# Moving the third chunk's inverse forward among the set-up work of a chunked RWKV-7 and GELU kernel

## Chip, core and metric

The kernel runs on one core of one Trainium2 chip, in fp32. The metric is the device time of one launch in microseconds (us). Five engines run their own queues in program order: PE (matrix multiply), DVE (vector), ACT (activations and copies), POOL (GpSimd) and SP, which here only issues transfers.

## What is computed

Two blocks follow each other. The first is a linear recurrence over 768 steps for 4 batches of 8 heads with a 40 x 40 state each, the second an MLP with exact GELU over 3072 tokens:

```python
for t in range(S):                                   # S = 768, state: (4, 8, 40, 40)
    y[:, :, t] = einsum('bhd,bhde->bhe', rt, state)
    Sa = einsum('bhde,bhe->bhd', state, at)
    state = state * wt[:, :, None, :] - einsum('bhd,bhe->bhde', Sa, bt)
    state = state + einsum('bhd,bhe->bhde', vt, kt)
x = y.transpose(0, 2, 1, 3).reshape(3072, 320)
h = x @ w_in                                          # 320 x 2048
out = (0.5 * h * (1 + erf(h / sqrt(2)))) @ w_out      # 2048 x 320
```

The two weight matrices arrive as 64-bit floats, so the kernel turns their words into fp32 itself, and this conversion is a large part of the set-up.

## The kernel before

**Chunks.** Time is cut into `NCH` = 12 chunks of 64 steps. Within a chunk the recurrence is solved by matrices. From the decays come `logs` (ACT, logarithm in place), `sums` (PE sums `cum` and `wT_ps`, then two exponentials on ACT), the scaled inputs `scale_b`, `scale_k`, `scale_a`, and their transposes `turn_a`, `turn_b`, `turn_k`, `turn_v`, `turn_r`. `make_N` multiplies the transposed a and b (`N_ps`), masks the product on DVE into `N` and writes its 32 x 32 blocks to DRAM. `start_inverse` fetches the blocks as `Nb` and inverts them column by column (L601, L603: two small elementwise operations for each of 31 columns), on DVE for chunk 0 and on POOL for the others. `store_inverse` and `fetch_inverse` take the result `W` through DRAM into `Tt` and `T2`; `turn_corner`, `corner` (`J`) and `joined` (the second `J`) complete it to 64 x 64. `make_A`, `make_av` and `make_RV` are further masked products. The serial part over the chunks is `make_X`, `make_sa`, `make_saT`, `make_y2`, `make_M`, `make_QY` and `outputs`, which writes the next state and the MLP's input `xt`.

**The MLP in pieces.** `mlp(c)` (L781) is a generator of eight pieces for each chunk: four pieces of the first layer (`ph`, one GELU on ACT each, into `gt`), then four of the second layer (`po`, 16 matmul records each; the first two pieces use rows 0 to 7 of `w_out_sb`, the last two rows 8 to 15). `fill()` puts the next piece of the oldest open chunk into PE's queue.

**Weight words.** `first_load` brings words of `w_in`, `first_convert` turns one (row block, half) into fp32: five pieces for the first half, five for the second. In this text they are called pieces 0 to 4 and h0 to h4. The first half's words wait in `w_out_sb` (not yet needed), the second half's in `gt` and `spare_raw`. `second_load` and `second_convert` do the same for the sixteen row blocks f0 to f15 of `w_out`. `to_float` (L281) uses DVE for the bit operations, ACT for a rescaling, and then either DVE or POOL for the last two operations; `power` and `mant` have two buffers each. `convert(n)` and `seconds(n, loads)` take the next n pieces from `queue`; a piece finished on DVE is begun one piece ahead.

**What sets the order.** The order on every engine is the order in which the program is written, by a manual schedule; there is no planner. L848 to L1012 are the set-up, written out by hand: chunks 0, 1 and 2 and the preparation of chunk 3, with conversions and MLP pieces of chunk 0 placed between. From L1014 a loop runs over c = 2 to 11, with eight `fill()` in each pass. Eight transfers can be open at once: each transfer issued by SP waits for the landing of the one eight earlier, as well as for its data and its target. PSUM has four tiles of the size `duo`, which all matrix results share.

**Names near the change.** `nb_ring`, `wp_ring`, `part_ring`, `avs_ring` hand out fixed buffers in turn. `raws` holds what was fetched. In the set-up before, chunk 2 is fetched by L886 (w) and L915, L916 (a, b); `sums(2)` is L940, `make_N(2)` L951, `run(start_inverse(2, ...))` L960; the first-half pieces are at L894 to L918, the second half's at L938 to L955; f0 to f15 at L966 to L1005; `store_inverse(2)` is L1000, `make_N(3)` L1007.

Of the kernel before, what the change touches and what calls it, by code (L numbers as in the profile page):

```python
# [19 lines left out]
def kernel(  # L20
# [197 lines left out]
    spare_raw = work.tile([P, 4 * DM], UINT32, tag="spare", name="spare_raw")  # L218
    early_a = spare_raw.bitcast(FP32).rearrange("p (n d) -> p n d", d=BW)

    for t in w_tile, early_w:
        nc.gpsimd.memset(t[:, G * DM:], 0.0)
    load_w(0)
# [137 lines left out]
    def second_load(f, slot, at=late_raw):  # L361
# [4 lines left out]
            to = second_raw[f] = at[:, slot * DM:(slot + 2) * DM]  # L366
        nc.sync.dma_start(out=to, in_=src[f * P:(f + 1) * P])

    def second_convert(f, eng):
        if wide_out:  # L370
            yield from to_float(w_out_sb[:, f], second_raw.pop(f), eng)
# [7 lines left out]
    def run(steps):  # L379
        for _ in steps:  # L380
            pass


    decays, turned_in = {}, {}
# [5 lines left out]
    def sums(c):  # L390
        logw = raws.pop((c, "w"))
        cum = duo("cum")[:, :, :DM]
        for g in range(G):
            mm(cum[:, g], cum_m, logw[:, g * DM:(g + 1) * DM])

        pt = duo("wT_ps").rearrange("p e (n t) -> p e n t", t=C)
        for n in range(G * NP):
            for x in range(2):
                for e in range(2):
                    at = (2 * n + x) * D  # L400
                    mm(pt[half(x), e, n], logw[half(e), at:at + HP], cum_m[half(e), half(e)])
        rw = (avs_ring if c in (1, 2) else part_ring)()[:, :, :DM]
        nc.scalar.activation(rw, cum, ACT.Exp, scale=-1.0)
        wp = wp_ring()
        nc.scalar.activation(wp[:, :, 1:].rearrange("p (n e) t -> p e n t", e=2), pt, ACT.Exp)
        decays[c] = rw.rearrange("p g (h d) -> p g h d", h=H), wp

# [11 lines left out]
    def side(name, tag, bufs):  # L419
        return work.tile([P, G, NP, P], FP32, tag=tag, name=name, bufs=bufs)  # L420
# [10 lines left out]

    def scale_b(c):
        rwv, wp = decays[c]
        nb = nb_ring()
        nc.vector.scalar_tensor_tensor(nb[:, :, :, :D], raws.pop((c, "b")), -1.0, rwv, ALU.mult, ALU.mult)
        turned_in.setdefault(c, {}).update(nb=nb, wp=wp)

# [20 lines left out]

    def turn_b(c):
        t = turned_in[c]  # L460
        nT = side("nT", "nT", 1)
        nc.scalar.copy(nT, flip(by_pair(t["nb"]), "nT_ps"))
        t["nT"] = parts(nT)

    def turns_a(c):
        turn_a(c)
        scale(c)
        scale_a(c)
        turn_b(c)

    def turn_k(c):
        t = turned_in[c]
# [3 lines left out]

    def turn_v(c):
        t = turned_in[c]
        vT = side("vT", "late", 1)
# [46 lines left out]

    blocks = {}

    def make_N(c):
# [9 lines left out]
        masked(flat(N), products("N_ps", t["nT"], t["aT"], True))  # L539
        blk = dram.tile([2, 2, 2 * G * NP, BL, BL], FP32, tag="N", name="N")  # L540
        for j in range(2):
            for z in range(2):
                at = j * HP + z * BL
                nc.sync.dma_start(out=blk[j, z].rearrange("n s t -> s n t"),
                                  in_=flat(N)[at:at + BL, :, z * BL:(z + 1) * BL])
        blocks[c] = blk
# [19 lines left out]
        t = turned_in[c]  # L566
        masked(flat(t["A"]), t.pop("A_ps"))

    def make_av(c):
        t = turned_in[c]  # L570
        av = duo("av")[:, :, :G * NP * D].rearrange("p x (g i d) -> p x g i d", g=G, i=NP)
        for g, i, x, e, q, m in units():
            mm(av[half(e ^ x), x, g, i], t["A"][half(e), x, g, i], t["VR"][half(e), g, q, m, :D])
        avs = t["avs"] = avs_ring()
        nc.scalar.copy(avs[:, :, :DM], av.rearrange("p x g i d -> p x (g i d)"))  # L575


    inverses = {}
# [107 lines left out]
    def make_sa(c):  # L686
# [176 lines left out]
    turn_b(1)  # L863
    scale_k(0)
    make_N(1)

    spare_x = work.tile([P, NK, TB], FP32, tag="xt", name="spare_x").rearrange("p k t -> p (k t)")
    st_ring()
# [25 lines left out]
    first_pieces((0,), 0, nc.vector)  # L894
    convert(1, True)
    mask_A(1)
    logs(2)
    first_load(True, 0, early(4))
    first_load(False, 2, early(5, 4))
    corner(0)  # L900
    joined(0)
    first_pieces((1, 2), 0, nc.gpsimd)
    first_pieces((3,), 0, nc.vector)
    first_pieces((4,), 0, nc.gpsimd)
    convert(1, True)
    make_X(0)
    make_sa(0)
    make_saT(0)
    convert(1, True)
    make_y2(0)  # L910
    make_M(0)
    store_inverse(1)
    load_r(1)
    fetch_inverse(1)
    load_a(2)  # L915
    fetch(2, "b", b, nc.sync)  # L916
    first_load(False, 3)
    convert(1, True)  # L918
    make_QY(0)
    outputs(0)  # L920
    pieces.append(mlp(0))
    make_av(1)
    corner(1)
    convert(1, True)
    joined(1)
    turn_state()
    make_X(1)
    turn_v(1)
    turn_r(1)
    make_RV(1)  # L930
    for f in range(2):
        second_load(f, 2 * f)
    first_load(True, 1, spare_raw[:, :LW])
    fetch(2, "k", k, nc.sync)
    for f in range(2, 8):
        second_load(f, 2 * f)

    first_pieces(range(NK), 1, nc.gpsimd)  # L938
    convert(1)
    sums(2)  # L940
    convert(1)
    make_sa(1)
    make_saT(1)
    scale_b(2)
    turn_a(2)
    scale_a(2)
    convert(1)
    fill()
    turn_b(2)
    fill()  # L950
    make_N(2)  # L951
    convert(1)
    make_y2(1)
    make_M(1)
    convert(1, True)  # L955
    scale_k(2)
    nc.gpsimd.memset(spare_st.rearrange("p e i g d -> p (e i g) d")[:, :, D:], 0.0)
    for n in "av":
        unused(paired[n], nc.gpsimd)
    run(start_inverse(2, nc.gpsimd))  # L960
# [12 lines left out]
    outputs(1)  # L973
    pieces.append(mlp(1))
    turn_v(2)
# [8 lines left out]
    fetch(3, "k", k, nc.sync)  # L984
    load_VR(3)
    load_a(3)
    seconds(1, (11, 14))
    fill()
    seconds(1, (12, 0, spare_raw))
    seconds(1, (13, 2, spare_raw))  # L990
    make_av(2)
    sums(3)
    scale(3)
    turn_a(3)
    scale_a(3)
    turn_state()
    fill()
    seconds(2, (14, 14))
    turn_b(3)
    store_inverse(2)  # L1000
    fetch_inverse(2)
    seconds(1, (15, 0, spare_raw))
    load_r(3)
    load_v(3)
    seconds(2, last=True)  # L1005
    fill()
    make_N(3)  # L1007
    run(start_inverse(3, nc.gpsimd))
    turn_k(3)
    turn_r(3)  # L1010
    turn_corner(2)
    fill()  # L1012
# [87 lines left out]
```

## Time and profile before

| what | value |
|---|---|
| time, median of 3 runs | 774.02 us (770.8 to 774.39) |
| the profiled execution | 767.67 us, span on the core 765.9 us |
| PE matmul busy | 699.2 us, 91% of the span |
| DVE, ACT, POOL busy | 277.8, 218.7, 311.5 us |
| mean granted PE clock | 0.95 |
| bytes moved | 67.82 MB in 268361 packets |

The profiled execution is 3.1 us below the fastest of the three timed runs. The page's first part gives each engine's busy time; its second cuts the span into 40 slices of 19.1 us, a digit for tenths busy, with PE's granted clock in a row of its own. Other views used below are the stretches (busy time of each engine between two times), the waits (who waited for whom), the timeline (instructions in order of time) and the chain of work that ended last. "<-" after a name reads "from": in `Tt<-inv` the tile `Tt` is loaded from `inv`, and "[6.62 <-DVE A L507]" says that the engine sat idle for 6.62 us until a DVE instruction of line 507 ended.

### The profile page before, as it was taken

Reading aid. Unit: us, or ns where it says so; the run is one execution under the profiler, and the core shown is the slowest. Engines: PE = TensorE matmul, PEld = TensorE weight load, DVE = VectorE, ACT = ScalarE, POOL = GpSimd, SP = SyncE. Lnnn points to the kernel's source line nnn. Section 1 sums busy time; section 2 is a strip of 40 time slices with the busy share of each in tenths; the row PEclk is TensorE's granted clock in tenths of the full one; section 3 lists DMA queues with packets and bytes.
Section 4 is the critical chain, followed back from the end, with each engine's and each line's share of the span. In section 5 each row is a group of like instructions: output and inputs, shape, how many; then the busy total and the mean of one; then the engine's idle time right before and its main releaser. Section 6 shows DMA issues by size and latency. Waiting matters only on the chain.

```text
span 765.9 us, 30557 instructions
## 1 busy us (share of the span) xinstructions
PE 699.2 (91%) x13792; PEld 561.3 (73%) x13792; DVE 277.8 (36%) x420; ACT 218.7 (29%) x262; POOL 311.5 (41%) x778
## 2 busy tenths in 40 slices
PE   7346787676999999999999999999999999999997
PEld 5346676454887877877878878878878878778684
DVE  3777456963143143243252242341241431321000
ACT  5124653340331331341332322322322413102020
POOL 3384248820750750841832823814804706500000
PEclk9666999886999999999999999999999999999999
DMA  9896565465725635535537337237347241110100
GB/s 117 137 174 133 117 195 98 89 127 120 128 45 99 117 69 101 100 66 115 94 59 130 72 68 142 58 69 135 63 76 138 50 74 38 34 36 3 27 9 17
DMA packets 268361, 67.82 MB, mean 89 GB/s; under 512 B 256616, under 2 KB 261512, under 8 KB 268232
## 3 DMA queue, kind: packets, MB, share of 16 engines
q1 hardware_dynamic: 268032, 65.71, 45.9%
q8 instruction: 108, 1.77, 1.0%
q14 instruction: 21, 0.17, 0.1%
q10 hardware_dynamic: 200, 0.16, 0.1%
HBM read 51.68 MB, written 10.22 MB: 81 GB/s over the span
## 4 chain that ended last, share of the span: by engine, by line
PE 77%; POOL 7%; SPq 5%; issue 5%; DMA 4%; DVE 1%; ACT 0%; POOLq 0%; DVEq 0%; ACTq 0%
PE po L797 26%; PE ph L789 26%; PE QY L100 5%; PE J L100 2%; PE N_ps L100 2%; POOL tmp L601 1%; POOL W L603 1%; PE sap L100 1%; PE X L100 1%; DMA a_pairs<-in_a_dram 1%; POOL st L603 1%; PE saT_ps L100 1%; PE kT_ps L413 1%; PE nT_ps L413 1%; PE cum L100 1%
## 5 line engine op out<-in xcount | busy, mean ns | idle before, releaser
L797 PE MATMUL po<-w_out_sb,gt 128*128 128x320 f32 x768 | 223.8, 444 | 17.0 <-DVE w_out_sb L297 15.3
L789 PE MATMUL ph<-xt,w_in_sb 64*128 64x256 f32 x1920 | 223.7, 385 | 5.3 <-POOL w_in_sb L302 4.8
L789 PEld LDWEIGHTS ph<-xt,w_in_sb 64*128 64x128 f32 x1920 | 184.9, 189 | 29.6 <-POOL w_in_sb L302 5.6
L797 PEld LDWEIGHTS po<-w_out_sb,gt 128*128 128x128 f32 x768 | 144.0, 193 | 79.7 <-DVE w_out_sb L297 20.6
L601 POOL TENSOR_TENSOR tmp<-W,Nb 128x126 f32<-128x126 f32 (+22 forms) x310 | 111.6, 360 | 172.8 <-DMA Nb<-N 149.2
L603 POOL TENSOR_TENSOR W<-W,tmp 128x126 f32<-128x126 f32 (+22 forms) x310 | 118.6, 383 | 24.3
L791 ACT ACTIVATE gt<-ph 128x1024 f32<-128x1024 f32 x48 | 49.2, 1024 | 166.3 <-PE ph L789 166.2
L801 DVE COPY os<-po 128x320 f32<-128x320 f32 x24 | 11.8, 491 | 108.7 <-PE po L797 108.7
L507 DVE TENSOR_TENSOR SM<-M_ps,upper 128x1024 f32<-128x1024 f32 x12 | 14.7, 1224 | 67.6 <-PE M_ps L100 67.5
L591 POOL MEMSET W<- 128x512 f32 x10 | 5.3, 530 | 73.8 <-DMA inv<-W 73.8
L746 DVE TENSOR_TENSOR xt<-QY,wpT 128x512 f32<-128x512 f32 x24 | 15.4, 685 | 51.3 <-PE QY L100 51.3
L668 DVE COPY Tt<-J 32x512 f32<-32x512 f32 x12 | 8.3, 689 | 67.5 <-ACT Tt L668 67.5
L474 ACT COPY kT<-kT_ps 128x1024 f32<-128x1024 f32 x12 | 12.1, 1011 | 70.9 <-PE kT_ps L413 70.9
L507 DVE TENSOR_TENSOR VR<-RV_ps,upper 128x1024 f32<-128x1024 f32 x12 | 14.7, 1222 | 43.1 <-PE RV_ps L100 43.1
L441 POOL TENSOR_TENSOR ks<-k_raw,part 128x640 f32<-128x640 f32 x10 | 16.2, 1617 | 32.5 <-DMA k_raw<-in_k_dram 17.2
L507 DVE TENSOR_TENSOR A<-A_ps,upper 128x1024 f32<-128x1024 f32 x12 | 14.6, 1220 | 39.4 <-PE A_ps L100 39.4
L289 ACT ACTIVATE power<-power,rebias 128x320 uint32<-128x320 uint32 (+1 forms) x26 | 16.0, 622 | 44.8 <-DVE power L288 44.8
L791 ACT ACT_TABLE_LOAD x10 | 12.8, 1283 | 43.6 <-PE ph L789 43.6
L575 ACT COPY avs<-av 128x640 f32<-128x640 f32 x12 | 8.3, 693 | 53.5 <-PE av L100 53.5
L100 PE MATMUL QY<-SM,nb 64*64 64x104 f32 x768 | 21.3, 263 | 1.3 <-DVE SM L507 1.3
L100 PEld LDWEIGHTS QY<-SM,nb 64*64 64x64 f32 x768 | 18.7, 140 | 5.1 <-issue 3.6
L100 PEld LDWEIGHTS av<-VR,A 64*64 64x64 f32 x768 | 13.9, 149 | 11.6 <-DVE A L507 6.8
(152 smaller groups left out, 878.0 us busy)
## 6 DMA issues: line engine op xcount, KB each, us to landing
Nb<-N SPq DMA_DIRECT2D x22, 256.0 KB
VR<-in_v_dram SPq DMA_DIRECT2D x24, 160.0 KB
out_dram<-os SPq DMA_DIRECT2D x48, 80.0 KB
w_tile<-in_w_dram SPq DMA_DIRECT2D x22, 160.0 KB
b_raw<-in_b_dram SPq DMA_DIRECT2D x22, 160.0 KB
k_raw<-in_k_dram SPq DMA_DIRECT2D x22, 160.0 KB
w_out_sb<-in_moe_w_out_dram SPq DMA_DIRECT2D x11, 320.0 KB
N<-N SPq DMA_DIRECT2D x48, 64.0 KB
```

The source lines that it names most:

```text
L100: nc.tensor.matmul(o, lhsT, rhs, start=first, stop=True, skip_group_check=True)
L289: nc.scalar.activation(power, power, ACT.Relu, bias=rebias, scale=8.0)
L413: nc.tensor.transpose(pt[:, g, n], src(g, n), ident)
L441: eng.tensor_tensor(ks[:, :, :, :D], raws.pop((c, "k")), rwv, ALU.mult)
L474: nc.scalar.copy(kT, flip(by_pair(t["ks"]), "kT_ps"))
L507: nc.vector.tensor_tensor(to, pt, upper.unsqueeze(1).to_broadcast([P, 2 * G * NP, C]), ALU.mult)
L601: eng.tensor_tensor(t, W[:, :rows, j:j + 1].to_broadcast([P, rows, rest]), Nb[:, j:j + 1, j + 1:].to_broadcast([P, rows, rest]), ALU.mult)
L603: eng.tensor_tensor(W[:, :rows, j + 1:], W[:, :rows, j + 1:], t, ALU.add)
L746: nc.vector.tensor_tensor(xt[:, :NP, g * P:(g + 1) * P].rearrange("p i (e t) -> p i e t", e=2), Y, wp[:, g, :, :, :C], ALU.mult)
L789: nc.tensor.matmul(ph[:, x, s], w_in_sb[half(x), kt, p * P:(p + 1) * P], xt[half(x), kt], start=kt == 0, stop=kt == NK - 1)
L791: nc.scalar.activation(gt[:, 4 * q:4 * q + 4].rearrange("p (x s) t -> p x s t", x=2), ph, ACT.Gelu)
L797: nc.tensor.matmul(po[:, g], gt[:, f, g * P:(g + 1) * P], w_out_sb[:, f], start=f == 0, stop=f == NF - 1)
```

## The change

Line numbers are those of the kernel before. The change touches the order of the set-up and some buffers.

- Chunk 2's decays, transposes and `N` product move forward. `load_w(2)`, `load_a(2)` and `fetch(2, "b")` are issued ahead of the first weight words; `logs(2)`, `sums(2)`, `turn_a(2)` stand ahead of `run(inverse)`, the rest (`scale_b`, `turn_b`, `scale_a`, the product of `make_N`) between `fetch_inverse(0)` and `corner(0)`. Two temporary buffers hold its results: `wp_2` in `spare_raw` and `nb_2` in the tile of `a`. `move(2)` copies them into the rings later, on ACT. The exponential for chunk 2 goes to `part_ring`; chunk 1's `make_X` writes over its `avs`.
- All four parts of the first half's words are issued later, the first after `fetch_inverse(0)`. All five first-half pieces are finished on POOL, and all stand after `make_M(0)`.
- The inverse of chunk 2 is started before the first conversions and its 31 columns are spread: 10 after piece 4, 2 after h1, the rest after h4.
- Three more loads of `w_out` words (f10, f11, f15) get buffers of their own. Two `fill()` of the set-up are taken away, and f14 and f15 are converted in the loop's first pass.
- `make_N(3)` now stands ahead of `store_inverse(2)`, and `store_inverse(2)` and `fetch_inverse(2)` directly ahead of chunk 3's `start_inverse`.
- In the loop's first pass two second-layer pieces of chunk 0 come after `make_saT(2)`, with pieces of chunk 1's first layer ahead of them (`pieces.reverse()`), and the pass has ten `fill()`.

```diff
+    wp_2 = spare_raw.bitcast(FP32)[:, :G * NP * 2 * (C + 1)].rearrange("p (n t) -> p n t", t=C + 1)
+    nb_2 = by_64(paired["a"]).rearrange("p (g h) d -> p g h d", g=G)
...
+    def columns(n):
+        for _ in range(n):
+            next(later, None)
...
-        rw = (avs_ring if c in (1, 2) else part_ring)()[:, :, :DM]
+        rw = (avs_ring if c == 1 else part_ring)()[:, :, :DM]
-        wp = wp_ring()
+        wp = wp_2 if c == 2 else wp_ring()
...
-        nb = nb_ring()
+        nb = nb_2 if c == 2 else nb_ring()
...
+    def move(c):
+        t = turned_in[c]
+        nb, wp = nb_ring(), wp_ring()
+        nc.scalar.copy(nb[:, :, :, :D], t["nb"][:, :, :, :D])
+        nc.scalar.copy(wp[:, :, 1:], t["wp"][:, :, 1:])
+        t["nb"], t["wp"] = nb, wp
+        decays[c] = decays[c][0], wp
...
-        xs = t["xs"] = part_ring()
+        xs = t["xs"] = t["avs"] if c == 1 else part_ring()
...
-    fetch(1, "k", k, nc.sync, ahead["k"])
+    load_w(2)
     load_VR(0)
     load_r(0)
-    first_load(False, 0, early(0, 4))
-    first_load(False, 1)
+    load_a(2)
+    fetch(2, "b", b, nc.sync)
     turn_k(0)
     make_A(0, False)
+    logs(2)
     turn_v(0)
     turn_r(0)
     make_RV(0, False)
+    sums(2)
+    turn_a(2)
     run(inverse)
     store_inverse(0)
-    load_VR(1)
-    load_w(2)
+    fetch(1, "k", k, nc.sync, ahead["k"])
     fetch_inverse(0)
+    mask_A(0)
+    scale_b(2)
+    make_av(0, False)
+    turn_b(2)
+    scale_a(2)
     scale_k(1, nc.vector)
-    mask_A(0)
+    copy_av(0)
     mask_RV(0)
-    make_av(0)
+    make_N(2, False)
     turn_k(1)
     make_A(1, False)
-    first_pieces((0,), 0, nc.vector)
-    convert(1, True)
     mask_A(1)
...
+    first_load(False, 0, early(0, 4))
+    store_inverse(1)
+    first_load(False, 1)
     corner(0)
     joined(0)
+    mask_N(2)
+    load_VR(1)
+    first_pieces(range(NK), 0, nc.gpsimd)
     make_X(0)
     make_sa(0)
     make_saT(0)
+    fetch_inverse(1)
+    first_load(True, 0, early(4))
+    later = start_inverse(2, nc.gpsimd)
+    first_load(False, 2, early(5, 4))
     make_y2(0)
     make_M(0)
+    convert(2)
     make_QY(0)
     outputs(0)
     pieces.append(mlp(0))
     make_av(1)
     corner(1)
+    convert(1)
     joined(1)
+    move(2)
+    convert(1)
     turn_state()
     make_X(1)
+    convert(1, True)
+    first_load(False, 3)
+    load_r(1)
...
+    columns(10)
+    first_pieces(range(NK), 1, nc.gpsimd)
+    make_sa(1)
+    make_saT(1)
+    convert(1)
+    fill()
+    convert(1)
+    fill()
+    turn_v(1)
+    turn_r(1)
+    make_RV(1)
+    columns(2)
+    convert(1)
     make_y2(1)
     make_M(1)
+    convert(2, True)
     scale_k(2)
...
+    columns(BL)
...
+    second_load(10, 0, words("b_raw"))
+    second_load(11, 0, words("k_raw"))
+    second_load(15, 0, words("rT", 2))
     second_pieces(range(NF), nc.vector)
-    seconds(3)
+    seconds(2)
     fill()
     turn_k(2)
+    make_QY(1)
     fill()
-    seconds(3)
-    make_QY(1)
+    seconds(2)
     outputs(1)
...
     load_w(3)
-    fetch(3, "b", b, nc.sync)
-    seconds(2, (10, 12))
-    logs(3)
...
+    seconds(4, (12, 12))
     load_VR(3)
     load_a(3)
+    logs(3)
     make_av(2)
     sums(3)
+    seconds(1, (13, 14))
+    fill()
+    seconds(3)
+    fetch(3, "b", b, nc.sync)
+    fetch(3, "k", k, nc.sync)
+    turn_a(3)
+    turn_state()
+    seconds(2, (14, 14), last=True)
     scale(3)
     scale_a(3)
+    turn_b(3)
     fill()
+    make_N(3)
     store_inverse(2)
     fetch_inverse(2)
+    run(start_inverse(3, nc.gpsimd))
...
     for c in range(2, NCH):
         corner(c)
         make_X(c)
+        if c == 2:
+            pieces.reverse()
+            seconds(2, last=True)
+            turn_r(n)
         fill()
...
         make_saT(c)
+        if c == 2:
+            pieces.reverse()
+            fill()
         fill()
         make_y2(c)
         make_M(c)
+        if c == 2:
+            fill()
```

More of the change, by code (lines that the diff above doesn't have):

```diff
@@ L367, in second_load, with words @@
         nc.sync.dma_start(out=to, in_=src[f * P:(f + 1) * P])
+    def words(tag, bufs=1):
+        return work.tile([P, 2 * DM], UINT32, tag=tag, name="words", bufs=bufs)
     def second_convert(f, eng):
@@ L460, in turn_b @@
         t = turned_in[c]
-        nT = side("nT", "nT", 1)
+        nT = side("nT", "late" if c == 2 else "nT", 1)
         nc.scalar.copy(nT, flip(by_pair(t["nb"]), "nT_ps"))
         t["nT"] = parts(nT)
[L465 to L469, printed above, removed]
+    def move(c):
[5 more added lines that the diff above has]
+        decays[c] = decays[c][0], wp
     def turn_k(c):
@@ L478, in turn_v @@
         t = turned_in[c]
-        vT = side("vT", "late", 1)
+        vT = side("vT", "kT" if c == 1 else "late", 1)
         if c < NT:
@@ L527, with make_N, mask_N @@
     blocks = {}
-    def make_N(c):
+    def make_N(c, mask=True):
+        t = turned_in[c]
+        t["N_ps"] = products("N_ps", t["nT"], t["aT"], True)
+        if mask:
+            mask_N(c)
+    def mask_N(c):
         t = turned_in[c]
@@ L538, in make_N @@
         t["N"] = N
-        masked(flat(N), products("N_ps", t["nT"], t["aT"], True))
+        masked(flat(N), t.pop("N_ps"))
         blk = dram.tile([2, 2, 2 * G * NP, BL, BL], FP32, tag="N", name="N")
@@ L567, in mask_A, with make_av @@
         masked(flat(t["A"]), t.pop("A_ps"))
-    def make_av(c):
+    def make_av(c, copy=True):
         t = turned_in[c]
@@ L573, in make_av, with copy_av @@
             mm(av[half(e ^ x), x, g, i], t["A"][half(e), x, g, i], t["VR"][half(e), g, q, m, :D])
+        t["av_ps"] = av.rearrange("p x g i d -> p x (g i d)")
+        if copy:
+            copy_av(c)
+    def copy_av(c):
+        t = turned_in[c]
         avs = t["avs"] = avs_ring()
-        nc.scalar.copy(avs[:, :, :DM], av.rearrange("p x g i d -> p x (g i d)"))
+        nc.scalar.copy(avs[:, :, :DM], t.pop("av_ps"))
     inverses = {}
@@ L865 @@
     make_N(1)
+    nc.gpsimd.memset(wp_2[:, :, 0], 1.0)
     spare_x = work.tile([P, NK, TB], FP32, tag="xt", name="spare_x").rearrange("p k t -> p (k t)")
@@ L882 @@
     make_RV(0, False)
+    sums(2)
+    turn_a(2)
     run(inverse)
     store_inverse(0)
-    load_VR(1)
-    load_w(2)
+    fetch(1, "k", k, nc.sync, ahead["k"])
     fetch_inverse(0)
+    mask_A(0)
[3 more added lines that the diff above has]
+    scale_a(2)
     scale_k(1, nc.vector)
-    mask_A(0)
+    copy_av(0)
     mask_RV(0)
-    make_av(0)
+    make_N(2, False)
     turn_k(1)
     make_A(1, False)
-    first_pieces((0,), 0, nc.vector)
-    convert(1, True)
     mask_A(1)
-    logs(2)
-    first_load(True, 0, early(4))
-    first_load(False, 2, early(5, 4))
+    first_load(False, 0, early(0, 4))
+    store_inverse(1)
+    first_load(False, 1)
     corner(0)
     joined(0)
[L902 to L905, printed above, removed]
+    mask_N(2)
+    load_VR(1)
+    first_pieces(range(NK), 0, nc.gpsimd)
     make_X(0)
@@ L908 @@
     make_saT(0)
-    convert(1, True)
+    fetch_inverse(1)
+    first_load(True, 0, early(4))
+    later = start_inverse(2, nc.gpsimd)
+    first_load(False, 2, early(5, 4))
     make_y2(0)
     make_M(0)
[L912 to L918, printed above, removed]
+    convert(2)
     make_QY(0)
@@ L923 @@
     corner(1)
-    convert(1, True)
+    convert(1)
     joined(1)
+    move(2)
+    convert(1)
     turn_state()
     make_X(1)
+    convert(1, True)
+    first_load(False, 3)
+    load_r(1)
+    first_load(True, 1, spare_raw[:, :LW])
+    for f in range(2):
+        second_load(f, 2 * f)
+    fetch(2, "k", k, nc.sync)
+    for f in range(2, 8):
+        second_load(f, 2 * f)
+    columns(10)
[5 more added lines that the diff above has]
+    convert(1)
+    nc.gpsimd.memset(spare_st.rearrange("p e i g d -> p (e i g) d")[:, :, D:], 0.0)
+    fill()
     turn_v(1)
@@ L930 @@
     make_RV(1)
[L931 to L951, printed above, removed]
+    columns(2)
     convert(1)
@@ L954 @@
     make_M(1)
-    convert(1, True)
+    convert(2, True)
     scale_k(2)
-    nc.gpsimd.memset(spare_st.rearrange("p e i g d -> p (e i g) d")[:, :, D:], 0.0)
     for n in "av":
         unused(paired[n], nc.gpsimd)
-    run(start_inverse(2, nc.gpsimd))
+    columns(BL)
     load_VR(2)
@@ L980 @@
     load_w(3)
-    fetch(3, "b", b, nc.sync)
-    seconds(2, (10, 12))
-    logs(3)
-    fetch(3, "k", k, nc.sync)
+    seconds(4, (12, 12))
     load_VR(3)
     load_a(3)
[L987 to L990, printed above, removed]
+    logs(3)
     make_av(2)
     sums(3)
+    seconds(1, (13, 14))
[6 more added lines that the diff above has]
+    seconds(2, (14, 14), last=True)
     scale(3)
-    turn_a(3)
     scale_a(3)
-    turn_state()
+    turn_b(3)
     fill()
-    seconds(2, (14, 14))
-    turn_b(3)
+    make_N(3)
     store_inverse(2)
     fetch_inverse(2)
-    seconds(1, (15, 0, spare_raw))
+    run(start_inverse(3, nc.gpsimd))
     load_r(3)
     load_v(3)
[L1005 to L1008, printed above, removed]
     turn_k(3)
-    turn_r(3)
     turn_corner(2)
-    fill()
     for c in range(2, NCH):
```

## The prediction

> **What bounds the kernel now.** I read the slices first, then stretches, PE's waits, and the timelines of PE, POOL and SP.
>
> ```profile
> PE   7346787676999999999999999999999999999997
> PEclk9666999886999999999999999999999999999999
> ```
>
> PE and its clock reach 9 in the eleventh slice (about 191 us) and stay there. So only the set-up can win or lose. The stretches (busy us of PE, PEld, DVE, ACT, POOL; clock; DMA share; GB/s) show how:
>
> ```profile
> 44.00:62.00 18.00, 6.40 (x224) 5.68 (x228) 11.96 (x20) 4.72 (x6) 14.10 (x34) 0.60 0.78 143
> 62.00:97.00 35.00, 26.43 (x953) 23.46 (x944) 21.86 (x33) 18.88 (x30) 10.81 (x9) 0.84 0.69 138
> 97.00:133.00 36.00, 29.71 (x500) 24.54 (x502) 21.48 (x35) 15.71 (x23) 22.56 (x37) 0.93 0.61 144
> 133.00:193.00 60.00, 42.73 (x582) 28.91 (x578) 39.10 (x77) 17.50 (x24) 21.85 (x47) 0.77 0.57 112
> ```
>
> After 97 us, PE's longest waits are for converted weights:
>
> ```profile
> PE po L797 <- DVE w_out_sb L297: 15.3, 7, 6.7
> PE ph L789 <- POOL w_in_sb L302: 4.8, 2, 3.1
> ```
>
> The timeline gives the marks that I move (start, duration):
>
> ```profile
> 42.65 1.16 PE L100 MATMUL RV_ps<-rT,vT 40*64 40x64 f32 x64 [1.10 <-ACT rT L495]
> 50.43 1.95 PE L100 MATMUL av<-VR,A 64*64 64x40 f32 x64 [6.62 <-DVE A L507]
> 60.12 1.08 PE L100 MATMUL J<-L,N 32*32 32x32 f32 x64 [3.54 <-DVE L L638]
> 138.72 1.15 PE L100 MATMUL A_ps<-aT,kT 40*64 40x64 f32 x64
> 191.83 1.14 PE L100 MATMUL X<-st,aT 40*64 40x40 f32 x64
> ```
>
> X of chunk 2 ends at 193.0; from there PE is full to the end. My method: find when the changed kernel ends that X, add PE work that it still owes there. Eight MLP pieces are done by then before, six after, so two second-layer pieces (4.50 and 4.31 in the chain's rows at 218.85 and 227.48) are owed: +8.8. The change must therefore end X by 184.2 to break even.
>
> **What the Trainium skill says.** "TensorE: Matmul & The Clock Gate", Part 1: an idle PE falls to half clock and needs sustained work to return. The trace agrees: 0.60 in 44 to 62, and `QY` from `SM` took 3.05 at 71.65 but 1.66 at 129.79. "SBUF — State Buffer", Who interferes with whom: a DVE instruction with two SBUF inputs contends with a GpSimd instruction that reads SBUF. It agrees: a second-layer conversion starts every 2.74 (142.65 to 145.39) beside POOL's columns, every 1.93 (163.13 to 165.06) without. "ScalarE: Activation LUTs", What ACT_TABLE_LOAD costs: 1283 ns for any set; here 1.28. "DMA: Bandwidth & Descriptors", Anatomy of one DMA: about 2 us fixed, on the GpSimd path; on SP's the chain shows 2.02 for a block store of `N` and 3.40 for `inv`.
>
> **Part 1: chunk 2's N in the wait.** PE idles from 43.8 to 50.4. But `sums(2)` can't start there: in the changed order `cum` waits for chunk 0's A mask, which empties the PSUM tile it takes, and that mask stands behind DVE's inverse (done 48.3). So the new work starts at 49.4 and lies on the way to the first J, not beside it. Durations from before's rows, slow ones because the clock was 0.53:
>
> - PE: cum 2.5 (154.02) to 52.0; wT_ps 1.4 to 53.5; a's flips 2.0 (as kT at 52.30) to 55.3.
> - ACT beside it: table 1.28, exponentials 0.70 and 1.03, to 55.0.
> - DVE: `scale_b` writes into a's tile, so it waits for the flips: 0.83 to 56.2; `scale_a` to 57.3, `scale_k(1)` 1.05 to 58.3, RV mask to 59.4.
> - PE: av to 57.2, b's flips to 58.7, ACT copy 1.0 to 59.7, N to 61, k's flips 2.0 to 62.8, copy to 63.9, A to 65.3; DVE mask 1.2 and corner transpose 0.7 to 67.2.
>
> J starts at 67.3 instead of 60.12: +7. With all these at full clock (cum 1.34, flips 1.04 and so on) I get +3; with another table load and slow products +9. I take +7. The moved `N` (1.2), flips and sums cost PE nothing later; before they sat at 88 to 109 between waits, so little is won there.
>
> SP: the first words are issued after `fetch_inverse(0)`, at about 55.5 instead of 37.1; w, a and b of chunk 2 (0.98 MB in all) and k of chunk 1 take their place. Behind that queue the fourth words part is issued at 95 instead of 80.5, landing by an estimated 102 (before 7 to 8 after issue).
>
> **Part 2: first half on POOL.** J's second product, sap, saT, M follow as before, 7 later; QY ends at 83 (76.3). Pieces 0 and 1 run beside QY. Then DVE and ACT take turns: one piece holds DVE 1.5, ACT 1.9 to 2.0, POOL 2.65 (L301 1.29 and L302 1.35). `move(2)` adds 0.7 and 1.0 on ACT, ahead of piece 3 on that queue. POOL ends piece 4 at about 99.3 (before 84.8). The first two `ph` still end near 106.4 (before 107.9), because sums, a, b and RV work no longer precede them.
>
> **Part 3: columns between conversions.** Ten columns take POOL 8.5 (before, 8.1 quiet at 31.88 and 9.4 at 124.11), to 107.8. h0 follows to 110.5. The first GELU writes where h0's words lie, so it waits for POOL at 109.1; behind it in ACT's queue stand h1's rescaling, then the v and r copies, for which RV waits. h1 ends at 114.9, two columns (2.0) at 117.3. RV at 116.6, its mask to 119, h2 to 124.5, h3 to 128, h4 to 130.7. Before h4 ended at 119.1. The other 19 columns run 134 to 155.5; before the inverse ended at 155.2. So the inverse is not earlier; the conversions are 11.6 later. The third `ph` waits for h4: it ends at 133.3, QY(1) at 137.6 (132.9), the fourth `ph` 142.5, A of chunk 2 148.8 (139.9): +9.
>
> **Part 4: the second layer's conversions.** Before, f0 to f4 were done ahead of `xt`; now f0 to f2, as f0 needs the `mant` buffer h3 leaves. DVE idles for RV until 147.8; masks and a memset to 151.1. Then f3 and f4 at 2.7, f5 to f10 at 1.93: 168.1. Transpose of a 1.25; f11 to f13 5.3 to 174.6; `scale_b(3)` to 175.4. PE meanwhile waits: `sums(3)` needs `logs(3)`, which is behind f7's rescaling on ACT, so PE idles some 9 us before 160; the word load for f12 holds SP until f6 is done, but what stands behind it (v, a) lands in time. The buffers for f10, f11 and f15 remove before's 6.26 wait for `spare_raw` (timeline at 177.56); DVE is late for another reason, so I book nothing more. After `scale_b(3)`: flips 1.1, one po piece 4.5, N 1.1, mask to 183.5.
>
> **Part 5: N(3) ahead of the inverse's store.** Before:
>
> ```profile
> 166.87 1.28 SPq L615 DMA_DIRECT2D inv<-W  x2
> 170.94 1.93 SPq L625 DMA_DIRECT2D Tt<-inv  x4
> 185.51 1.93 SPq L544 DMA_DIRECT2D N<-N  x4
> ```
>
> The fetch was long over at J(2). Now SP waits for the N(3) mask, writes N (1.93), stores (1.28, 3.4 to land), fetches (two of four needed, 2.8 to land), and DVE transposes 0.7: 9.5 after the mask. PE has only k's flips (1.1) in that time. J(2) 193, X ends at 194.9.
>
> **Sum.** X is +1.9; the two owed pieces +8.8; after a 10 us wait PE is slow again, +0.8 (the po piece after before's wait took 5.33, not 4.50). Total +11.5. Against its own execution: 767.67 + 11.5 = 779.2. That execution is 6.35 below the median of its runs, so the same difference on 774.02 gives 785.5. From the bounds, J +3 to +9, POOL's columns 8.1 to 9.4, the fetch 8 to 12 and an uncertainty of some 4 in the DVE chain give 778 to 793.
>
> **Rivals.**
>
> 1. *Faster.* POOL had room: in 60 to 121 it waited 19.3 and 16.0 for ACT's `mant`. If the twelve columns (10.5) fit into such waits and J is only 3 late, h4 ends at 116, not 130.7. Each microsecond of h4 is one of N(3) and X, so X ends about 14.5 earlier; f3 and f4 without POOL beside them save 1.6: total -4.5, 769.5. It decides for faster when h4 ends before about 119. Against it: POOL waits for ACT because ACT waits for DVE and for GELU, and the program puts ten columns in one block ahead of h0.
> 2. *Level.* h4 ends near 119 to 122 and the inverse's fetch lies partly beside po: 774.
> 3. *Much slower.* The words are the bound: the fourth part lands after 108 and the second layer's loads queue behind it. DVE starts h0 some 6 later and every following step with it: +18, 792; with the longer J bound 797.
> 4. *It does not do what it says*, that is, the wait of the first transfers is not used: this is inside my forecast, since `cum` waits for DVE.
>
> **Numbers.** Forecast 60%, much slower 12%, level 14%, faster 14%. Likeliest time 785.5, its own range 778 to 793. For 8 in 10 I reach down to 772 (some 10% beneath) and up to 797. A measurement of this kernel can tell 0.5%, 3.9 us, from no change: faster 0.14, same 0.14, slower 0.72.
>
> **What would show it.** J of chunk 0 at 67 rather than 60; L302's fifth run on POOL at 98 to 100; h4 at 131; a PE wait of about 9 us for DVE's L just before J(2), which before was hidden; X(2) ending near 195; po no longer waiting for L297 by more than a few us. I am wrong if h4 ends before 122, if J(2) follows N(3) directly, or if PE is full before 185.

## The result, and the profile after

The changed kernel takes 794.4 us, median of 4 runs (791.01 to 796.12), against 773.52 us (4 runs, 770.8 to 774.39) for the kernel before: a ratio of 1.0271, 95% interval 1.0227 to 1.0314. That is 20.9 us slower, where 11.5 were forecast. Its profiled execution took 793.85 us (span 792.0), near its median. In later series the kernel before ran between 767.83 and 777.87 us (one run of 783.74 at a lower clock is left out), so its profiled 767.67 was at the fast end of its runs; that is why the spans differ by 26.1 us and the medians by 20.9.

The slices of the changed kernel, as on its page:

```profile
PE   7366666854799999999999999999999999999997
PEclk9676785968699999999999999999999999999999
```

A slice is 19.8 us here. PE is at 9 from the twelfth slice on, and the loss lies ahead of that. The same stretches as before (busy us of PE, PEld, DVE, ACT, POOL; clock; DMA share; GB/s):

```profile
44.00:62.00 18.00, 10.83 (x284) 8.53 (x272) 10.04 (x18) 4.80 (x6) 15.10 (x39) 0.81 0.56 108
62.00:97.00 35.00, 21.91 (x850) 20.15 (x854) 19.98 (x28) 15.79 (x26) 11.56 (x12) 0.70 0.66 136
97.00:133.00 36.00, 23.85 (x393) 19.95 (x386) 12.13 (x19) 15.15 (x22) 22.71 (x36) 0.69 0.70 157
133.00:193.00 60.00, 38.44 (x590) 30.39 (x592) 40.58 (x83) 19.83 (x27) 22.02 (x46) 0.76 0.35 81
```

The first stretch did fill: PE 10.83 instead of 6.40. The three behind it hold 14.7 us less PE work in all (84.2 against 98.9), and the clock in 97 to 133 fell from 0.93 to 0.69. PE's longest waits after 97 us:

```profile
PE J L100 <- DVE L L664: 9.3, 1, 9.3
PE nT_ps L424 <- DVE nb L446: 8.6, 1, 8.6
PE cum L100 <- ACT w_tile L399: 8.0, 1, 8.0
PE RV_ps L100 <- ACT rT L509: 5.7, 2, 4.6
PE ph L815 <- POOL w_in_sb L305: 5.1, 2, 3.8
```

Before, PE waited for converted second-layer weights (15.3 us in seven waits). That is gone; in its place stand three waits of 8 to 9 us: `cum` for chunk 3's logarithm, the flips of b (`nT_ps`) for its scaled b, and J for chunk 2's corner. The marks, from PE's timeline:

```profile
66.00 1.08 PE L100 MATMUL J<-L,N 32*32 32x32 f32 x64 [1.96 <-DVE L L664]
153.97 1.11 PE L100 MATMUL A_ps<-aT,kT 40*64 40x64 f32 x64
203.83 1.08 PE L100 MATMUL J<-L,N 32*32 32x32 f32 x64 [9.25 <-DVE L L664]
204.84 1.95 PE L100 MATMUL X<-st,aT 40*64 40x40 f32 x64
206.71 7.40 PE L815 MATMUL ph<-xt,w_in_sb 64*128 64x256 f32 x40
```

What J waited for is in SP's queue. The three kinds of transfer that the prediction's part 5 shows now stand in the other order, the inverse's store and fetch behind the blocks of `N`:

```profile
194.88 1.94 SPq L564 DMA_DIRECT2D N<-N  x4
196.91 1.28 SPq L641 DMA_DIRECT2D inv<-W  x2
200.51 1.90 SPq L651 DMA_DIRECT2D Tt<-inv  x4
```

X of chunk 2 ends at 206.8 instead of 193.0: 13.8 us. The rest of the span is longer too, as the stretches from the end of X to the end show, the kernel before first, then the changed one:

```profile
193.00:765.90 572.90, 566.98 (x11080) 458.58 (x11080) 157.61 (x194) 146.51 (x166) 222.48 (x590) 1.00 0.39 74
```

```profile
206.80:792.00 585.20, 578.34 (x11112) 465.51 (x11112) 163.70 (x207) 148.15 (x168) 223.94 (x590) 1.00 0.39 75
```

The 32 additional matmul records are the two owed pieces. 13.8 + 12.3 = 26.1, the whole difference of the spans. In what follows, "the rest" is this stretch from the end of X of chunk 2 to the end.

### The profile page after: what moved, and what is told of

The parts are those of the page before. It is cut to its first block, busy times and chain, and to the rows that moved or that the text cites. A ratio compares the mean times of both kernels' runs of the same rounds, so it can differ in the third digit from the quotient of the medians.

```text
span 792.0 us, 30573 instructions
## 1 busy us (share of the span) xinstructions
PE 704.3 (89%) x13792; PEld 568.2 (72%) x13792; DVE 273.0 (34%) x416; ACT 222.5 (28%) x268; POOL 314.6 (40%) x783
## 4 chain that ended last, share of the span: by engine, by line
PE 78%; POOL 5%; DMA 5%; DVE 4%; SPq 3%; issue 3%; ACT 2%; POOLq 0%; DVEq 0%; ACTq 0%
PE ph L815 27%; PE po L823 26%; PE QY L100 6%; PE J L100 2%; PE cum L100 2%; POOL st L629 2%; POOL st L627 2%; PE nT_ps L424 2%; PE RV_ps L100 1%; PE X L100 1%; PE N_ps L100 1%; PE sap L100 1%; PE saT_ps L100 1%; PE av L100 1%; PE kT_ps L424 1%
## 5 line engine op out<-in xcount | busy, mean ns | idle before, releaser
L815 PE MATMUL ph<-xt,w_in_sb 64*128 64x256 f32 x1920 | 228.0, 391 | 5.4 <-POOL w_in_sb L305 5.1
L823 PE MATMUL po<-w_out_sb,gt 128*128 128x320 f32 x768 | 217.2, 437 | 2.3 <-DVE os L827 2.3
L815 PEld LDWEIGHTS ph<-xt,w_in_sb 64*128 64x128 f32 x1920 | 187.0, 192 | 31.8 <-POOL w_in_sb L305 6.6
L823 PEld LDWEIGHTS po<-w_out_sb,gt 128*128 128x128 f32 x768 | 142.8, 190 | 60.8 <-DVE os L827 4.4
L629 POOL TENSOR_TENSOR W<-W,tmp 128x126 f32<-128x126 f32 (+22 forms) x310 | 116.8, 377 | 24.3
L521 DVE TENSOR_TENSOR SM<-M_ps,upper 128x1024 f32<-128x1024 f32 x12 | 14.7, 1224 | 69.1 <-PE M_ps L100 69.1
L772 DVE TENSOR_TENSOR xt<-QY,wpT 128x512 f32<-128x512 f32 x24 | 15.4, 685 | 56.3 <-PE QY L100 56.3
L521 DVE TENSOR_TENSOR VR<-RV_ps,upper 128x1024 f32<-128x1024 f32 x12 | 14.7, 1224 | 44.9 <-PE RV_ps L100 44.9
L521 DVE TENSOR_TENSOR A<-A_ps,upper 128x1024 f32<-128x1024 f32 x12 | 14.7, 1223 | 43.5 <-PE A_ps L100 43.5
L100 PE MATMUL cum<-w_tile,cum_m 128*128 128x320 f32 x44 | 16.6, 506 | 13.7 <-ACT w_tile L399 8.0
L100 PEld LDWEIGHTS cum<-w_tile,cum_m 128*128 128x128 f32 x44 | 9.6, 223 | 18.7 <-ACT w_tile L399 8.1
```

The costliest lines, as they stand in the source:

```text
L100: nc.tensor.matmul(o, lhsT, rhs, start=first, stop=True, skip_group_check=True)
L521: nc.vector.tensor_tensor(to, pt, upper.unsqueeze(1).to_broadcast([P, 2 * G * NP, C]), ALU.mult)
L629: eng.tensor_tensor(W[:, :rows, j + 1:], W[:, :rows, j + 1:], t, ALU.add)
L772: nc.vector.tensor_tensor(xt[:, :NP, g * P:(g + 1) * P].rearrange("p i (e t) -> p i e t", e=2), Y, wp[:, g, :, :, :C], ALU.mult)
L815: nc.tensor.matmul(ph[:, x, s], w_in_sb[half(x), kt, p * P:(p + 1) * P], xt[half(x), kt], start=kt == 0, stop=kt == NK - 1)
L823: nc.tensor.matmul(po[:, g], gt[:, f, g * P:(g + 1) * P], w_out_sb[:, f], start=f == 0, stop=f == NF - 1)
```

## Experiments

All but the last start from the changed kernel. Each series had runs of the kernel before beside it (medians 771.93, 773.98 and 773.66 us). The number behind each time is the ratio to them, with its 95% interval; it is not the quotient of the medians. The changed kernel was not run again in the series, and the interval of every single edit but one overlaps its own, 1.0227 to 1.0314; only undoing part 1 lies above it, and only the kernel with several edits together lies below. So for the single edits the trace decides what happened, not the time.

The traces have a spread too. The changed kernel and five of the edited ones (the store ahead of N(3), the three tries with the owed pieces, and the two first edits together) are alike up to N(3), yet in their profiles h4 ends at 132.1 to 136.4 us and the flips of b begin at 182.7 to 187.6. A mark that moves by less than 5 us from one profile to another shows nothing by itself. Stretches within one profile repeat better. From the moment DVE is free for f3 to the end of `scale_b(3)` takes 26.99 to 27.44 us in all six. The rest takes 584.5 to 586.1 us in the changed kernel and five others that leave the owed pieces where the change has them and in which J waits as long for L.

**Inverse's store ahead of N(3).**

```diff
-    make_N(3)
     store_inverse(2)
     fetch_inverse(2)
+    make_N(3)
```

> The changed kernel with store_inverse(2) and fetch_inverse(2) written ahead of make_N(3) instead of behind it. Theory A (the way through DRAM behind N's mask is on the path): in the changed kernel J of chunk 2 starts 10.2 after the kT flips began (193.49 to 203.83), 9.25 of it a wait for the transpose L. The inverse was ready at 156.5, so the transfer now ends beside the flips and J follows them at 195 to 196: 8 to 9 us less than the changed kernel's 794.4, about 786. Rival B (PE must wait there anyway, for N(3)'s mask, PSUM or the transfer behind the last word load that holds SP until 184.7): the wait becomes one for another thing and the gain is under 3 us, 791 or more.

788.9 us, 1.0229 [1.0151, 1.0307]. J follows at once, but a new wait appears in the loop:

```profile
193.86 0.74 PE L100 MATMUL J<-L,N 32*32 32x32 f32 x64 [1.03 <-DVE L L664]
208.94 1.83 PE L100 MATMUL sap<-part,Tt 64*64 64x40 f32 x59 [3.32 <-DVE Tt L694]
```

X ends at 195.7, 11.1 earlier. Of this 8.2 is the wait, 1.15 is that J and X ran at full clock (0.74 and 1.14 us instead of 1.08 and 1.95), and 1.75 is spread: the flips of k began that much earlier in this profile, before the edit takes effect. The rest is 4.6 longer (589.8 us). PE waits 3.3 of it because the corner's copy to `Tt` stands on DVE behind r's transpose, which waited 6.68 for r to land (`load_r(3)` is issued late in this order), and what follows that wait ran slow again (the next `po` 5.75 us instead of 4.57). Theory A holds for the wait; the median shows 5.5 us of it.

**The owed pieces put back, first try, and both edits.** The two pieces and the conversions of f14 and f15 come behind `turn_k(3)`, with `turn_r(3)` ahead of the pieces; the reversals and the extra `fill()` of the loop's first pass go.

```diff
     turn_k(3)
+    seconds(2, last=True)
+    turn_r(3)
+    fill()
+    fill()
     turn_corner(2)
```

> The changed kernel with the two owed second-layer pieces taken out of the loop again and put, with the conversions of f14 and f15, behind turn_k(3), where the changed kernel's PE waits 9.25 us. Theory A (the owed pieces cost their own 8.8 us because PE idles while they could run): J of chunk 2 stays at 203 to 206, and the loop is shorter by two pieces, and PE comes to the loop at full clock: 8 to 12 us less than 794.4, 783 to 786. Rival B (the pieces were owed because their weights are late): f14 and f15 hold the second piece and the corner's transpose, J moves to 208 or later, and the gain is under 4 us.

> The first two edits together. Theory A says that both use the same wait of PE behind N(3): with the transfer early J could follow the flips, and the two pieces stand ahead of it, so the sum is not 17 to 21 us but about that of one, 9 to 12 us less than 794.4, 782 to 785. If they use different waits the gains add up, to 775 or less.

798.71 us (1.0348 [1.0279, 1.0416]) alone, 795.63 us (1.0301 [1.0233, 1.0368]) with the store ahead. Both expectations missed. DVE's timeline of the first says why:

```profile
211.79 1.25 DVE L167 STREAM_TRANSPOSE rT<-r_pairs 128x1024 f32<-128x1024 f32 x1 [12.15 <-DMA v_pairs<-in_v_dram]
212.96 0.45 DVE L827 COPY os<-po 128x320 f32<-128x320 f32 x1
```

My own edit put r's transpose ahead of the copy that frees the piece's output, and PE idled 12.96 us between the two pieces (8.60 with the store ahead). The line names a load of v, which stands directly behind those of r on SP. So X came late, and the total time says nothing on what the owed pieces cost. The rest does, here for the first kernel and for both edits together:

```profile
223.25:797.00 573.75, 566.91 (x11080) 458.13 (x11080) 157.75 (x194) 146.71 (x166) 211.26 (x559) 1.00 0.39 74
222.20:795.50 573.30, 566.85 (x11080) 458.19 (x11080) 157.58 (x194) 146.66 (x166) 210.78 (x556) 1.00 0.40 74
```

It is back near the 572.9 of the kernel before. The second try left `turn_r(3)` in the loop:

> The two owed second-layer pieces behind turn_k(3) again, as in e2_po_back, but turn_r(3) stays in the loop's first pass as the changed kernel has it. In e2_po_back the transpose of r stood on DVE ahead of the copy that frees the pieces' PSUM, and waited until 211.8 for r, so PE idled 12.96 us between the pieces. Theory A (the pieces fill the wait behind N(3) when nothing else stands there): J at 204 to 206, time 8 to 12 under 794.4, 783 to 786. Rival B (the pieces cost as much where they are put): within 3 us of 794.4.

797.04 us, 1.0301 [1.0264, 1.0339]; the rest is 575.0 us, but PE waits 12.21 us for J. There is one buffer `os`; its output transfer was queued on SP behind the sixteen loads of r and v, and the corner's transpose behind the second copy:

```profile
216.17 0.49 DVE L827 COPY os<-po 128x320 f32<-128x320 f32 x1 [15.58 <-DMA out_dram<-os]
216.57 0.70 DVE L664 STREAM_TRANSPOSE L<-Tt 128x512 f32<-128x512 f32 x1
```

**Third try, with the way clear.**

```diff
-    load_r(3)
-    load_v(3)
     turn_k(3)
+    seconds(2, last=True)
+    fill()
     turn_corner(2)
+    fill()
+    load_r(3)
+    load_v(3)
```

with `turn_r(3)` behind `make_M(2)`, and the reversals and extra `fill()` of the loop's first pass gone as before. At that place chunk 4's r has already been loaded into the tile, so chunk 3's products with r are made from chunk 4's; number and shapes of the instructions stay.

> The two owed second-layer pieces behind turn_k(3) for the third time, now with nothing else in their way: load_r(3) and load_v(3) behind them, so that their output transfers are not queued on SP behind sixteen loads; the corner's transpose between their two PSUM copies; turn_r(3) only after make_M(2). Theory A (the pieces are owed, and cost their own time in the loop, because PE idled while they could run): J of chunk 2 at 204 to 206 as in the changed kernel, time 8 to 12 under 794.4, 783 to 786. Rival B (whatever is put there takes up the gain): 791 or more.

787.35 us (783.37 to 792.19), 1.0224 [1.0164, 1.0283]. J starts at 202.95 without a wait, and the rest is the shorter one again:

```profile
202.95 0.75 PE L100 MATMUL J<-L,N 32*32 32x32 f32 x64
```

```profile
204.80:781.40 576.60, 568.15 (x11080) 458.95 (x11080) 160.16 (x196) 146.55 (x166) 222.70 (x590) 1.00 0.41 76
```

576.6 against 585.2: 8.6 us less for the two pieces and the slow clock behind the wait, and X ends no later than in the changed kernel. So in all four kernels that take the pieces out of the loop the rest is 8.6 to 11.9 us shorter, and in this one they fit into PE's wait. As to where the time goes, theory A holds. How much of it a whole launch gains is less sure: the profiled execution is the fastest of the four, the median is 7 us under the changed kernel's, and the ratio only 0.5%, with overlapping intervals. A kernel that does this and keeps chunk 3's r was not built.

**Columns behind h4.** `columns(10)` and `columns(2)` deleted.

> The changed kernel with all 31 columns of chunk 2's inverse behind h4 (none between conversions). Theory A of the prediction (the columns hold POOL's conversions back): h0 starts on POOL at about 100 instead of 109.2, h4 ends 10 to 12 earlier than 134.5, the inverse ends at 155 to 157 as before, and the time falls by about 9, to 785. Rival B (h0's words are late: DVE could not start h0 before they landed at 106.6): h0 on POOL starts at 109, only the two columns after h1 are won, h4 ends 2 or less earlier, the inverse ends at 166 and the time stays within 3 us of 794.4.

796.13 us, 1.0312 [1.0248, 1.0376]. The timelines of DVE and of POOL:

```profile
107.00 0.43 DVE L291 TENSOR_SCALAR power<-gt 128x512 uint32<-128x512 uint32 x1 [8.98 <-DMA gt<-in_moe_w_in_dram]
```

```profile
109.37 1.39 POOL L304 TENSOR_TENSOR mant<-mant,gt 128x512 f32<-128x512 f32 x1 [9.40 <-ACT mant L303]
```

POOL started h0 at 109.37 instead of 109.16, though it had nothing to do from 100 on. Rival B is right: h0's words are late, and the ten columns lie in POOL's wait for them. The prediction's reason against its first rival fell here. Nor are the columns free behind h4: there they run beside f3 and the pieces after it, and from f3 to `scale_b(3)` DVE took 29.1 us instead of 27.0.

**Words early, alone and with the columns last.** `first_load(False, 3)` directly behind `first_load(False, 2, ...)`.

> The changed kernel with the fourth part of the first half's words (first_load(False, 3)) issued directly behind the third, at about 88 instead of 99, the columns left where they are. Theory C (words and columns cover each other: the words landed at 106.6, POOL's ten columns ended at 107.5): DVE starts h0 at 97 to 100, but POOL reaches h0 only at 107.5, so h0 is 1 to 1.6 earlier and the time 0 to 2 under 794.4. Rival D (the words alone hold h0): h0 on POOL is over 4 earlier and the time under 790.

> Both: the words early and all columns behind h4. Theory C: only now does h0 move, to POOL at about 100 to 101 (109.2 in the changed kernel), h1 to 105. What comes next is RV(1): its r lands at about 112, so the mask that DVE has ahead of h2 comes 3 to 4 earlier, h4 ends at 130 to 131 instead of 134.5, and the time is 3 to 5 under 794.4, about 790. The inverse then ends at about 163, before the store at 197, so it costs nothing. Rival A (the columns' full 10 us come back): h4 at 124, time 785 or less. Rival E (the inverse is now late): over 794.

792.26 us (1.0243 [1.0212, 1.0273]) and 794.05 us (1.0269 [1.0235, 1.0302]). In the first, DVE began h0 at 99.93, but POOL only directly behind its columns, as theory C says:

```profile
99.93 0.43 DVE L291 TENSOR_SCALAR power<-gt 128x512 uint32<-128x512 uint32 x1 [3.23 <-DMA xt<-xt]
107.36 1.28 POOL L304 TENSOR_TENSOR mant<-mant,gt 128x512 f32<-128x512 f32 x1
```

In the second, POOL began h0 at 103.66 and ended h4 at 131.1, yet the time is that of the changed kernel and not the 790 expected: the columns now ran from 134.7 to 164.1 beside f3 to f5, which took 2.37 to 2.64 us a piece instead of 1.92, and from f3 to `scale_b(3)` DVE took 28.8 us instead of 27.0. So h4 and the columns trade places; both places cost.

**sums(3) later.**

```diff
     make_av(2)
-    sums(3)
     seconds(1, (13, 14))
     fill()
     seconds(3)
+    sums(3)
```

> The changed kernel with sums(3) written behind the conversions of f9 to f12 and the first piece of the second layer instead of ahead of them. In the changed kernel DVE stood still for 4.59 us before 173.35 because f9's rescaling lay on ACT behind the two exponentials of chunk 3, which wait for cum on PE. Theory F (this stall is on the path: scale_b(3), N(3), J follow DVE): scale_b(3) at 180 instead of 184.7, J at 199, time 4 to 6 under 794.4, 789 to 790. Rival G (the exponentials become late in turn and hold scale_b(3), or PE's order does): under 2 us.

790.19 us, 1.0227 [1.0191, 1.0262]; J at 200.74 (203.83). From f3 to `scale_b(3)` DVE took 22.8 us, where six profiles have 27.0 to 27.4: the stall is gone. The changed kernel had shown it as

```profile
173.35 0.49 DVE L296 SCALAR_TENSOR_TENSOR power<-spare_raw,power 128x320 uint32<-128x320 uint32 x1 [4.59 <-ACT power L292]
```

f9's rescaling lay on ACT behind two exponentials, those behind `cum`, that behind the logarithm. Theory F holds; the time falls by 3.4 us by the ratios and 4.2 by the medians.

**Part 1 undone.** `logs(2)`, `sums(2)`, the flips and scalings and `make_N(2)` between `joined(0)` and `make_M(0)`, or just behind it, and `start_inverse(2)` directly ahead of `columns(10)`.

> Part 1 of the change undone in the changed kernel: chunk 2's decays, flips and N come behind the first corner and before or behind make_M(0) instead of into the wait of the first inverse; the inverse is started just ahead of its first columns. Theory K (the prediction's part 1: J of chunk 0 is 6 late and everything after it): J at 60 to 61 instead of 66.0, but chunk 2's N, some 5 on PE and 4 on DVE, now lies ahead of the conversions; h4 and J of chunk 2 come 1 to 3 earlier, time 791 to 793. Rival L (the fourth words part at 106 and POOL's columns take up whatever comes early): J of chunk 0 at 60, h0 on POOL still at 108 to 110 and the time within 1.5 of 794.4. Under both, part 1 is worth little of the 20 us.

817.26 us, 1.0592 [1.054, 1.0644]. Both theories missed by over 20 us. J of chunk 0 did start earlier (61.87), but the fetch of N's blocks now stood on SP behind the word loads, was issued at 117.66, and POOL's ten columns waited for it with h0 behind them:

```profile
125.95 0.24 POOL L627 TENSOR_TENSOR tmp<-W,Nb 128x31 f32<-128x31 f32 x1 [20.64 <-DMA Nb<-N]
```

The edit moved a fetch besides what it was to move, so what part 1 is worth by itself stays open. It shows that columns ahead of conversions make POOL's queue hang on one transfer, here for 20.64 us.

**What helped, together.** Words early, `sums(3)` later, store and fetch of the inverse ahead of `turn_a(3)`, r and v ahead of `make_N(3)`, and the second po piece moved from ahead of N(3) to ahead of the flips of b.

> The edits that helped, together, in the changed kernel: the fourth words part early (e5, 2 less), sums(3) behind f9 to f12 (e7, 4 less), chunk 2's store and fetch of the inverse ahead of N(3) (e1, 5 to 6 less), load_r(3) and load_v(3) ahead of make_N(3) so that r's transpose doesn't hold DVE in the loop (3 less), and the second po piece moved from between the flips and N(3) into the 9 us that PE idles before those flips (4 to 5 less). If the causes are separate stretches of one chain they add up: 794.4 - 19 = 775, level with the kernel before, with only the two owed pieces (8.8) unpaid. If they overlap: 782 or more.

780.58 us, 1.0122 [1.0082, 1.0163]: 13.8 under the changed kernel, not 19. X ends at 190.1, within the spread of the kernel before's 193.0, so what the change had lost ahead of X is won back. The rest then takes 587.8 us, against 572.9: the two owed pieces (8.8), the first ph at slow clock (7.09 us instead of 4.59) and 1.6 for an output copy make 12.9 of these 14.9. Putting the owed pieces back in this version was not tried.

**One thing of the change in the kernel before.**

```diff
     second_load(9, 2, spare_raw)
+    second_load(15, 0, work.tile([P, 2 * DM], UINT32, tag="rT", name="words", bufs=2))
...
-    seconds(1, (15, 0, spare_raw))
+    seconds(1)
```

> The kernel before with one thing of the change: the words of f15 are loaded early into a buffer of their own (the free one of the two of rT) instead of late into spare_raw. In the kernel before DVE stood still 6.26 us before 177.56 for these words, and PE 6.71 at 179.5 for DVE. Theory M (that wait is on the path to N(3) and X of chunk 2): X ends at 187 instead of 193.0, time 5 to 6 under the kernel before. Rival N (the inverse's fetch, r's transpose or the outputs hold J at 190): under 2 us.

767.37 us, median of 22 runs (762.93 to 770.64); 0.9925 [0.9906, 0.9944]: 0.75% faster than the kernel before, with an interval clear of 1. DVE's wait in the kernel before, and PE's X in this one:

```profile
177.56 0.33 DVE L288 TENSOR_SCALAR power<-spare_raw 128x320 uint32<-128x320 uint32 x1 [6.26 <-DMA spare_raw<-in_moe_w_out_dram]
188.51 1.14 PE L100 MATMUL X<-st,aT 40*64 40x40 f32 x64
```

Theory M holds. From the end of A's product of chunk 2 to the end of X, 53.1 us became 46.9 (142.8 to 189.65), the 6.26 of DVE's wait. In its profiled execution A itself came 2.9 later than in the other, so X gained only 3.3 there.

## Why the prediction was right, and where not

It said slower, at 785.5 with a range of 772 to 797; 794.4 lies inside, but above the likeliest case's own 778 to 793. Median against median the change cost 20.9 us where 11.5 had been worked out. The working itself stands on profiles, and profile against profile it was 26.1, so it was off by 14.6 and not by 9.4. The smaller number is luck: the kernel before's profile was 6.35 under the median that was used, the changed kernel's 0.55. The working against the trace, in us; each column is one execution, and the marks from h4 on have the spread of 4 to 5 us that was shown above:

| mark | before | predicted | after |
|---|---|---|---|
| J of chunk 0 starts | 60.1 | 67.3 | 66.0 |
| POOL ends piece 4 | 84.8 | 99.3 | 99.5 |
| h4 ends | 119.1 | 130.7 | 134.5 |
| third ph ends | 123.7 | 133.3 | 140.0 |
| A's product of chunk 2 ends | 139.9 | 148.8 | 155.1 |
| DVE free for f3 | 142.6 | 151.1 | 158.6 |
| scale_b(3) ends | 158.1 | 175.4 | 185.6 |
| mask of N(3) ends | 185.5 | 183.5 | 194.8 |
| X of chunk 2 ends | 193.0 | 194.9 | 206.8 |
| rest to the end | 572.9 | 582.5 | 585.2 |

- **Part 1 held.** `cum` waited 5.78 for the A mask on DVE, began at 50.68, and J came 5.9 later (7 said). That this costs something at the end was argued, not shown.
- **Part 2 held.** POOL ended piece 4 at 99.5 (99.3 said); that it is so near is chance, since kernels alike up to there have it at 98.6 to 101.0.
- **Part 3 had the right place and the wrong causes.** h4 is 15.4 late, where 11.6 were said. The columns took 8.1 us (8.5 said), but removing them moved nothing. The fourth words part was issued at 99.1, behind the transfers of `xt`, and not at 95. It took 7.6 us to DVE, as before, so DVE had it at 106.7 instead of 102, and POOL began h0 at 109.2, 1.4 later than said. The columns alone would have let it begin at 107.5. This is the third rival's mechanism, in a small size. The larger loss lies between h2 and h3. PE stopped for 1.89 us in the middle of chunk 1's M, and DVE, which has M's mask ahead of h3, waited for it:

```profile
123.77 1.55 PE L100 MATMUL M_ps<-rT,saT 40*64 40x64 f32 x46 [1.89 <-issue]
125.37 1.23 DVE L521 TENSOR_TENSOR SM<-M_ps,upper 128x1024 f32<-128x1024 f32 x1 [2.72 <-PE M_ps L100]
```

In the seven kernels that have words and columns alike (the six above and that with `sums(3)` later), POOL's start of h0 to the end of h4 takes 24.5 to 26.9 us, and it grows about one for one with this stop, from 0.95 to 3.34 us. The prediction had 22.9 for it, and no stop. A further 2.9 was PE at slow clock: the last 24 records of the third ph took 5.49 us at a granted clock of 0.50, where 2.6 had been left for them. In the kernel before, the end of this ph had come 4.6 behind h4, at 0.63.

- **Part 4 was mis-sized by some 3** (DVE free for f3 to `scale_b(3)`: 27.0, 24.3 said). The wait ahead of `sums(3)` was 8.0 (9 said). What it did to ACT's queue was missed: f9's rescaling 4.59 late. 1.6 of that came back, since POOL was done at 156.7 and f3 and f4 took 1.92, not 2.7.
- **Part 5 held.** From the mask to J took 9.0 us (9.5 said), and the first experiment shows that 8.2 of them are this wait.
- **The owed pieces held**: 8.8 were booked, and in the four kernels without them in the loop the rest is 8.6 to 11.9 shorter, slow clock included. The slow clock was booked with 0.8 and is larger: the first ph behind J took 7.40 instead of 4.59, `po` 5.04 instead of 4.50, X 1.95 instead of 1.14.

So the direction was right, and the waits and the owed pieces were where the working had put them. The term that failed is "X is +1.9", which was +13.8. Of the 11.9 between them, 7.5 were lost before f3 (1.4 by the words, some 2.4 by M's stop and slow clock, 2.9 in the third ph, the remainder behind it), 2.7 in DVE's run to `scale_b(3)`, and 1.7 from there on, mostly slow clock. Which part of the 7.5 part 1 brought in stays open.

## What to carry to other kernels

When a transfer is moved behind others, look up when its data landed in the old trace and where it will stand in the queue; an engine that then seems to be the bound may only be waiting beside it. Each of the PE stalls of 3.3 to 13 us looked at here cost twice, once in the wait and once in the slow clock behind it, so the slow durations of the trace belong in the sum from the start. Before a mark is compared between two profiles, look how far it moves between kernels that are alike up to it; here that was 5 us. And of a change with many parts the useful one may be the smallest: here a buffer for one load, alone, gave 0.75%.

## What was not expected of the hardware

M of chunk 1 stopped at the same place in every kernel but the one with part 1 undone: after 18 of its 64 records (20 in the kernel before and in that with one buffer more), for a reason that the trace names only as "issue". The stop was 0.97 us before, 1.89 in the changed kernel, and 0.95 to 3.84 in the edited ones; the seven kernels above show it pass on to h4 about one for one.

And the slow clock outlasts a wait. Behind the 9.25 us wait at J the granted clock was 0.50 from 203.8 to 212.0 us and 1.00 from 213.0: J and X took 1.08 and 1.95 us, and the 40 records of the next ph 7.40 instead of 4.59. That is 8.6 us of slow time. In the five other kernels with the same wait of 9.3 us, it was 6.0 to 8.7. "TensorE: Matmul & The Clock Gate", Part 1: The HAM clock gate, in the Trainium skill puts the return at around 4 us of sustained matmul work; here PE, with work all the time, took half as long again to twice that.
